# A linear-attention block beside a gated MLP on one core: the last down forms made in one K step, and x's second chunk loaded into their place

## The chip, the cores and the metric

The kernel runs on one core of one Trainium2 chip. The metric is device microseconds of one execution. Before the change three runs took 726.26, 726.73 and 728.23 us, so the median is 726.73.

## What is computed

x has 2048 rows of 640 columns. Two branches read it and a gate mixes them row by row. Cut to what matters, the reference is:

```python
def _A_ref(x, wqkv, wo):                      # H = 32 heads of Dh = 20
    q, k, v = split_heads(x @ wqkv)
    phi = lambda t: jnp.where(t > 0, t + 1, jnp.exp(t)) + 1e-6
    pq, pk = phi(q), phi(k)
    kv = jnp.einsum("bhsd,bhse->bhde", pk, v)
    z = jnp.einsum("bhsd->bhd", pk)
    num = jnp.einsum("bhqd,bhde->bhqe", pq, kv)
    den = jnp.einsum("bhqd,bhd->bhq", pq, z)[..., None] + 1e-6
    return merge_heads(num / den) @ wo

def _B_ref(x, w_gate, w_up, w_down):          # F = 1536
    return (_sigmoid(x @ w_gate) * (x @ w_up)) @ w_down

g = _sigmoid((x * gate_w).sum(-1, keepdims=True))
out = g * _A_ref(x, wqkv, wo) + (1 - g) * _B_ref(x, w_gate, w_up, w_down)
```

## The kernel before, in words

**Arithmetic.** Every large product is made from fp32 operands split in two: ScalarE (ACT) copies the operand to a rounded high half (L420), VectorE (DVE) subtracts it to get the low half (L424), and TensorE (PE) makes three matmuls, high by high, high by low and low by high (`mm3`, L407 to L409). The products of 2 by 2 blocks are made in seven steps rather than eight, so sums and differences of blocks of x and of the weights are needed; these are called forms. A block of the K or the Q product goes through steps s1 to s7. Its sums stand in PSUM tiles named ch, dd, cc and rot, two slots each: a product on a slot waits until ACT or DVE has copied or added what the slot held.

**Stages.** The K phase goes through four chunks of x's rows (c = 0 to 3): the K products, phi, and a batch that accumulates K transposed times x (`GTBatch`, tiles gt). It needs blocks of 128 rows of x as they stand (tiles xnst, split into tok) besides the transposed chunks. Then comes the q phase of the first pair of row groups: 16 steps, with the small products of the attention placed into it by a table, `extra[j]`, where `kv_part` (L1630) makes a head group's kv from gt and wv, and `m_part` (L1641) multiplies kv by wo in six 320-wide matmuls on dd or cc, copies them to ms and stores them to m_dram. phi of q is made in `phi_q` (Exp and Relu on ACT, one DVE operation into qe, a store to p_dram). Then come the f phase of the first pair (12 blocks of F), the down products, and the same q and f phases for the other pair.

**What sets the order.** The order of the work on every engine is the order of the program. Some of it is written out by hand, the rest is decided by a planner at build time (class `Order`): it keeps estimated clocks of PE, ACT and DVE and queues of pieces of work, and lets a piece go when its turn comes (`run`), when something due needs it (`need`), or when there is room (`fill`). Loads are issued on SyncE's queue (SP), stores on GpSimd's (POOL); both take their instructions in order and a transfer that has to wait for its tile holds up those behind it. ACT, DVE and PE also work in order.

**Around the change.** `queue_ls` (L755) queues under the key "qw" the work for the last pair's down weights: two steps of sums, then four forms (j = 0 and 1, two halves each), in tiles qraw and qp; after the second half of each j two stores to the buffer wd go out on POOL's queue. In the third K step (c = 3, L1131 to L1240) the sums are run after s5, one form at a time afterwards, and `need("qw")` runs the rest. Then the pool that held these tiles is closed, and in their place tile xz (tag ws) takes most of x's second chunk of the first pair (`nx[1].load`: xm, then two transfers to xz), behind it goes a load of q weights (wg from wq). `queue_xn` splits the last row blocks, and `split_xn` loads a new block into xnst after a split. Later the tag ws is also used for weight tiles of the q products.

Of the kernel before, what the change touches and what calls it, by code (L numbers as in the profile page):

```python
# [9 lines left out]
AF = mybir.ActivationFunctionType  # L10
# [364 lines left out]
def gated_mix_kernel(ctx: ExitStack, tc: tile.TileContext, xt, xn, wk, wv, wo, wst_q, wst_f, out_t):  # L375
# [6 lines left out]
    order = Order()  # L382
# [3 lines left out]
    def f32(ap):  # L386
        return ap.bitcast(F32)

    def width(ap):
        n = 1  # L390
        for s in ap.shape[1:]:
            n *= s
        return n
# [24 lines left out]
    def act(out, src, fn, after="", **kw):  # L418
        order.on_act(width(out), after, out, src)
        nc.scalar.activation(out, src, fn, **kw)  # L420
# [368 lines left out]
    def queue_qw(u):  # L789

        raw = qs.tile([P, 2, D], F32, name="qraw", tag="qraw")
        sp.dma_start(raw, wst_q[:, u:u + 2])
        g, v = raw[:, 0], raw[:, 1]
        w = 2 * P

        def piece(i, c, src):
            n = width(src)

            def fn():
                t = qs.tile([P, 2, w], F32R, name="qp", tag="qp", bufs=2)  # L800
                split(t[:, 0, :n], t[:, 1, :n], src)
                order.then(lambda: sp.dma_start(w_dram["q", u, i][:, :, c:c + n], f32(t[:, :, :n])))
            order.add(a_cost(n), v_cost(n), fn, "qw",
                      None, kept=True)

        for i, n in enumerate((D, 3 * P, 9 * P)):
            w_dram["q", u, i] = dram.tile([P, 2, n], F32, name=f"wq{u}{i}")
        for i, src, c0 in ((0, g, 0), (1, v, w)):
            for c in range(c0, D, w):
                piece(i, c - c0, src[:, c:min(c + w, D)])  # L810
        a11, a12, a21, a22 = g[:, :w], g[:, w:2 * w], v[:, :w], v[:, w:2 * w]
        g5, v5 = g[:, 2 * w:], v[:, 2 * w:]

        def sums(part):
            if part == 0:
                add(a22, a21, a22)
                sub(a21, a11, a21)
            else:
                sub(a11, a22, a11)
                sub(a12, a12, a11)  # L820
                sub(g5, g5, v5)
        for part in range(2):
            order.add(0, 2 * v_cost(w), lambda part=part: sums(part), "qw", None, kept=True)
        for n, t in ((7, a22), (0, a11), (5, a21), (2, a12), (4, g5)):
            piece(2, n * P, t)
# [24 lines left out]
    def queue_xn(b):  # L850
        for n in (2 * b, 2 * b + 1):
            order.add(a_cost(D), v_cost(D), lambda n=n: split_xn(n), ("xn", b), lambda n=n: xn_st[n][1])
# [278 lines left out]
    for c in range(1, 4):  # L1131
        ck = chunks[c]
        if c == 1:
            queue_qw(2)
        a, b = KBlock(2 * c), KBlock(2 * c + 1)
        for n in range(1, 6):
            order.need((ck, n))
            if c == 1 and n >= 3:
                order.need(("ks", (1, 0, 2)[n - 3]))
            getattr(a, f"s{n}")()  # L1140
            getattr(b, f"s{n}")()
            for _ in range(({1: 1, 2: 1, 3: 1, 5: 1}, {5: 2})[c - 2].get(n, 0) if c > 1 else 0):
                order.run("qw")
        order.need((ck, 6))
        if c == 1:
            order.need(("ks", 5))
        if c == 2:
            chunks[c + 1].load()
        elif c == 3:
            nx = [Chunk(1, i, None, i * CW, xst_v, (b12h, b12l)) for i in range(2)]  # L1150
            nx[0].load()
        if c == 1:
            order.need(("xn", 1))
        queue_xn(2 * c)
        a.s6()
        a.s7()
        a.sum_b()
        a.phi_a()
        if c == 3:
            order.run("qw")  # L1160
            order.run("qw")
        b.s6()
        a.phi_b()
        order.need(("pk", 2 * c - 1))
        k_split(tok(2 * c, 0))
        b.s7()
        b.sum_b()
        k_split(tok(2 * c, 1))
        if c == 3:
            order.need("qw")  # L1170
            qs_cm.__exit__(None, None, None)
            pa_cm.__exit__(None, None, None)
            px_cm = tc.tile_pool(name="px", bufs=1, side="right", reuse_waits="tile")
            px = px_cm.__enter__()
            xf = XForms(px, TG)
            pg_cm = tc.tile_pool(name="pg", bufs=1, side="right", reuse_waits="tile")
            pg = pg_cm.__enter__()
            pz_cm = tc.tile_pool(name="pz", bufs=1, side="right", reuse_waits="tile")
            pz = pz_cm.__enter__()
            z = pz.tile([P, 8, CW], F32, name="xz", tag="ws")  # L1180
            z0 = m1_tile("ma", "xm")[:, :2 * CW].rearrange("p (k c) -> p k c", c=CW)
            nx[1].x = (Rows((0, 2, z0), (2, KC, z[:, 0:3])), z[:, 3:8])
            nx[1].load(((0, 0, 2), (0, 2, KC), (1, 0, KC)))
            W, WT = {}, {}

            def wg_tile():
                return pg.tile([P, 2, D], F32R, name="wg", tag="wg", bufs=2)

            def put(n, i, t):
                WT[n, i] = t  # L1190
                W[n, i] = [t[:, c] for c in range(2)]

            def store_w(n, i):

                key = n[::2] + (i,)
                w_dram[key] = dram.tile(list(WT[n, i].shape), F32, name="w%s%d%d" % key)
                gp.dma_start(w_dram[key], f32(WT[n, i]))

            def wg_split(n, src):
                put(n, 0, wg_tile())  # L1200
                split(*W[n, 0], src)
                if n[0] == "f" or n[2] == 0:
                    order.then(lambda: store_w(n, 0))
            nx[0].f = nx[1].f = xf
            put(("q", 1, 2), 0, wg_tile())
            sp.dma_start(f32(WT[("q", 1, 2), 0]), w_dram["q", 2, 0])
        g = GTBatch(c, batches[c])
        if c > 1:
            order.need(("xn", 2 * c))
        if c == 1:  # L1210
            chunks[1].store_t(1, 0)
        elif c < 3:
            chunks[c + 1].queue()
        else:
            queue_xn(7)
        first = 4 if c == 1 else 3
        for u in range(first):
            g.part(u, 0, 2, ("rot", "dd", "ch", "cc")[u])
            if c == 1 and u == 0:
                order.need(("xn", 2))  # L1220
                chunks[1].store_t(2, 3)
                chunks[2].queue()
            if u == (c == 1):
                b.phi_a()
            if u == 1 + (c == 1):
                b.phi_b()
                order.ahead(5)
        queue_split(2 * c + 1)
        if c < 3:
            queue_xn(2 * c + 1)  # L1230
        else:
            w_stage = m1_tile("ma", "w0")
            sp.dma_start(w_stage, wst_q[:, KC - 1])
            queue_forms(nx)
        if c == 3:
            for u in range(first, NU):
                g.part(u, 0, 2, ("cc", "dd", "rot", "cc")[u - first])
                order.fill()
            freed = [order.pe + P_LAG]
        for u in range(NU):  # L1240
            g.part(u, 2 if u in g.ps else 0, 4, ("rot", "dd", "ch", "cc", "dd", "rot", "rot")[u])
            order.fill()
            if u in (2, 3, 4, 6):
                order.run("qw")
            if c == 2 and u == NU - 1:
                queue_ls()
# [188 lines left out]
    def phi_q(g, u, src, after="p"):  # L1435

        n = phis.pop() + 1
        phis.append(n)
        order.need(("den", n - 2))
        e = tt("qe")  # L1440
        act(e, src, AF.Exp, after)
        r = src if after == "v" else tt("qr")
        act(r, src, AF.Relu)

        def rest():
            vec3(e, e, 1.0, r, OP.min, OP.add)
            gp.dma_start(p_dram[:, u, g], e)
            if g < 2:
                order.add(0, v_cost(TG), lambda: den_term(g, u, e), ("den", n), chain=True)
        order.need("phi")  # L1450
        order.follow(v_cost(TG), rest, "phi")
# [1032 lines left out]
    extra[0] += [lambda: queue_wo(1), lambda: queue_wo(0)]  # L2484
    extra[7].append(lambda: order.need((nx[1], 6), False))
    extra[9].append(lambda: order.need(("w", ("q", 1, 0), 1), False))
    for hg, (j, t) in enumerate(((5, "cc"), (6, "dd"), (8, "dd"), (10, "dd"), (12, "dd"), (13, "dd"))):
        extra[j].append(lambda hg=hg, t=t: m_part(hg, t))
    for hg, j in ((3, 8), (4, 9), (5, 10)):
        extra[j].append(lambda hg=hg: order.need(("wo", hg), False))  # L2490
    extra[13].append(lambda: order.need(("wg", ("f", 1, 0)), False))
    extra[13].append(lambda: order.need(("w", ("f", 1, 0), 0), False))
# [571 lines left out]
```

## Time and profile before

The profile is one execution with the hardware profiler on.

| | |
|---|---|
| median of three runs | 726.73 us |
| the profiled execution's own time | 726.68 us |
| its span, first to last instruction | 725.0 us |
| instructions | 9883 |
| granted clock of TensorE | 1.00 |
| PE busy, share of the span | 718.9 us, 99% |
| weight loads (PEld) | 606.2 us, 84% |
| DVE | 583.1 us, 80% |
| ACT | 371.1 us, 51% |
| POOL | 116.8 us, 16% |

Busy time of PE is time in which a matmul runs; consecutive matmuls overlap a little, so their starts, and not their durations, tell what one costs. A row of a timeline gives the start in us, the duration, the engine, the line, the operation with what it writes and reads, and in brackets how long the engine stood idle before it and what released it.

### The profile page before, as it was taken

The numbers are of one execution on the slowest core, as the hardware profiler recorded it, in microseconds if no ns is written. First come the engines' busy times: TensorE is split into PE (matmuls) and PEld (weight loads), VectorE is DVE, ScalarE is ACT, GpSimd is POOL, SyncE is SP. The second block draws the span as 40 slices with busy tenths as digits, with TensorE's granted clock in tenths as the row PEclk, the third lists the DMA queues.
The fourth block names the chain that finished last, engine by engine and source line by source line (L and its number), as shares of the span: only waits on it lengthen the run. The fifth ranks groups of instructions, "written<-read, shape, count | busy, mean of one in ns | idle before, by whom it ended". The sixth has DMA issues, their size and how long they took to land.

```text
span 725.0 us, 9883 instructions
## 1 busy us (share of the span) xinstructions
PE 718.9 (99%) x3395; PEld 606.2 (84%) x3395; DVE 583.1 (80%) x1009; ACT 371.1 (51%) x685; POOL 116.8 (16%) x189
## 2 busy tenths in 40 slices
PE   9999999999999999999999999999999999999998
PEld 8999998887788888888888888888888888888887
DVE  6888878788677989898989977447696968799895
ACT  5774748267556753636363764354423242444451
POOL 0211013123221212210210134001010101002300
PEclk9999999999999999999999999999999999999999
DMA  7677677978777866767687889968989895959957
GB/s 253 165 201 210 179 179 199 330 263 288 287 276 257 322 237 242 258 222 261 258 311 274 276 294 354 412 232 287 350 262 305 260 394 178 407 215 332 221 104 237
DMA packets 78889, 191.95 MB, mean 265 GB/s; under 512 B 8394, under 2 KB 37018, under 8 KB 75126
## 3 DMA queue, kind: packets, MB, share of 16 engines
q1 hardware_dynamic: 57654, 117.72, 49.2%
q0 software_dynamic: 20896, 73.36, 30.3%
q8 instruction: 27, 0.44, 0.2%
q10 hardware_dynamic: 288, 0.23, 0.1%
q14 instruction: 24, 0.20, 0.1%
HBM read 113.46 MB, written 75.52 MB: 261 GB/s over the span
## 4 chain that ended last, share of the span: by engine, by line
PE 91%; DMA 3%; issue 2%; DVE 2%; POOL 1%; ACT 1%; POOLq 0%; ACTq 0%; DVEq 0%
PE ch L407 10%; PE ch L408 10%; PE ch L409 10%; PE cc L407 8%; PE cc L408 8%; PE cc L409 8%; PE dd L407 6%; PE dd L408 6%; PE dd L409 6%; PE rot L407 5%; PE rot L409 5%; PE rot L408 5%; DMA wst<-wst_f 2%; DMA wst<-wst_q 1%; DMA p_dram<-qe 1%
## 5 line engine op out<-in xcount | busy, mean ns | idle before, releaser
L420 ACT ACTIVATE c<-ch 128x512 f32<-128x512 f32 x54 | 32.2, 596 | 80.1 <-PE ch L409 79.3
L424 DVE TENSOR_TENSOR hf<-c,hf 128x512 fp32r<-128x512 f32 x80 | 54.4, 686 | 19.4 <-ACT hf L420 18.9
L420 ACT ACTIVATE hf<-c 128x512 fp32r<-128x512 f32 x80 | 48.9, 624 | 31.1 <-DVE c L424 31.0
L424 DVE TENSOR_TENSOR c<-cc,c 128x512 f32<-128x512 f32 x42 | 28.9, 688 | 26.1 <-PE cc L409 16.6
L407 PE MATMUL ch<-xth,ws 128*128 128x512 f32 x112 | 43.9, 392 | 0.1
L408 PE MATMUL ch<-xtl,ws 128*128 128x512 f32 x112 | 43.7, 390 | 0.0
L409 PE MATMUL ch<-xth,ws 128*128 128x512 f32 x112 | 43.6, 389 | 0.0
L424 DVE TENSOR_TENSOR c<-c,c 128x512 f32<-128x512 f32 x52 | 35.7, 687 | 3.3 <-ACT c L420 2.7
L424 DVE TENSOR_TENSOR tb<-rot,tb 128x512 f32<-128x512 f32 x56 | 36.1, 680 | 0.4 <-PE rot L409 0.4
L407 PE MATMUL dd<-xrh,wg 128*128 128x512 f32 x90 | 35.2, 391 | 0.0
L408 PE MATMUL dd<-xrl,wg 128*128 128x512 f32 x90 | 35.0, 389 | 0.0
L409 PE MATMUL dd<-xrh,wg 128*128 128x512 f32 x90 | 35.0, 389 | 0.0
L420 ACT ACTIVATE c<-dd 128x512 f32<-128x512 f32 x22 | 13.1, 597 | 41.1 <-PE dd L409 41.1
L407 PE MATMUL cc<-xbh,ws 128*128 128x512 f32 x84 | 32.8, 390 | 0.5 <-DVE c L424 0.5
L408 PE MATMUL cc<-xbl,ws 128*128 128x512 f32 x84 | 32.7, 389 | 0.0
L409 PE MATMUL cc<-xbh,ws 128*128 128x512 f32 x84 | 32.7, 389 | 0.0
L424 DVE TENSOR_TENSOR tb<-dd,tb 128x512 f32<-128x512 f32 x36 | 24.7, 685 | 9.3 <-PE dd L409 9.3
L420 ACT ACTIVATE dd<-ch 128x512 f32<-128x512 f32 x22 | 12.8, 582 | 35.9 <-PE ch L409 35.9
L424 DVE TENSOR_TENSOR tb<-cc,tb 128x512 f32<-128x512 f32 x36 | 24.4, 683 | 1.9 <-PE cc L409 1.9
L424 DVE TENSOR_TENSOR wst<-wst 128x256 f32<-128x256 f32 (+1 forms) x65 | 24.6, 395 | 1.4
L407 PEld LDWEIGHTS ch<-xth,ws 128*128 128x128 f32 x112 | 21.0, 188 | 5.0 <-ACT c L420 0.9
L409 PEld LDWEIGHTS ch<-xth,ws 128*128 128x128 f32 x112 | 21.0, 188 | 4.7 <-DVE ws L424 0.3
(690 smaller groups left out, 2328.5 us busy)
## 6 DMA issues: line engine op xcount, KB each, us to landing
wf<-ws POOLq DMA_DIRECT2D x12, 1152.0 KB, 7.6
ws<-wf SPq DMA_DIRECT2D x11, 1152.0 KB, 7.8
wst<-wst_f SPq DMA_DIRECT2D x12, 640.0 KB, 5.3
wf<-wg POOLq DMA_DIRECT2D x12, 640.0 KB, 7.2
wd<-wd POOLq DMA_DIRECT2D x12, 640.0 KB, 7.8
wg<-wf SPq DMA_DIRECT2D x12, 640.0 KB, 6.6
wf<-wd SPq DMA_DIRECT2D x10, 640.0 KB, 10.4
xnst<-xn SPq DMA_DIRECT2D x16, 320.0 KB, 3.2
```

The costliest lines, as they stand in the source:

```text
L407: nc.tensor.matmul(out, l_hi, r_hi, start=first, stop=False, skip_group_check=True)
L408: nc.tensor.matmul(out, l_hi, r_lo, start=False, stop=False, skip_group_check=True)
L409: nc.tensor.matmul(out, l_lo, r_hi, start=False, stop=last, skip_group_check=True)
L420: nc.scalar.activation(out, src, fn, **kw)
L424: nc.vector.tensor_tensor(out, a, b, op=op)
```

## The change

Four places change.

1. In the third K step the queue "qw" is run four times after s5, not twice: the two sums and the first two forms (j = 0) follow each other.
2. The other two forms (j = 1) are run right after block a's s6 instead of after its `phi_a`.
3. In `phi_q`, when the source has been added by DVE (`after == "v"`), the planner is no longer told that Exp waits for DVE. That is a clock of the planner alone; the instruction still waits for its data.
4. m_part 5 moves from extra step 13 to 14, and the need for its wo block from step 10 to 11.

```diff
-            for _ in range(({1: 1, 2: 1, 3: 1, 5: 1}, {5: 2})[c - 2].get(n, 0) if c > 1 else 0):
+            for _ in range(({1: 1, 2: 1, 3: 1, 5: 1}, {5: 4})[c - 2].get(n, 0) if c > 1 else 0):
                 order.run("qw")
...
         a.s6()
+        if c == 3:
+            order.run("qw")
+            order.run("qw")
         a.s7()
         a.sum_b()
         a.phi_a()
-        if c == 3:
-            order.run("qw")
-            order.run("qw")
         b.s6()
...
-        act(e, src, AF.Exp, after)
+        act(e, src, AF.Exp, "" if after == "v" else after)
...
-    for hg, (j, t) in enumerate(((5, "cc"), (6, "dd"), (8, "dd"), (10, "dd"), (12, "dd"), (13, "dd"))):
+    for hg, (j, t) in enumerate(((5, "cc"), (6, "dd"), (8, "dd"), (10, "dd"), (12, "dd"), (14, "dd"))):
         extra[j].append(lambda hg=hg, t=t: m_part(hg, t))
-    for hg, j in ((3, 8), (4, 9), (5, 10)):
+    for hg, j in ((3, 8), (4, 9), (5, 11)):
         extra[j].append(lambda hg=hg: order.need(("wo", hg), False))
```

The order of the engines' instructions changes in several places, because the planner decides anew with every change of its clocks. On POOL's queue in the third K step, the stores of the forms (wd from qp and qraw) stand between accumulating stores of phi(k) (zacc from kr and kb); rows with - are the order before, with + the order now:

```order
 L364 DMA zacc<-kb 128x2x320
-L364 DMA zacc<-kr 128x2x320
 L364 DMA wd_1157<-qp 128x512
 L364 DMA wd_1157<-qraw 128x512
-L364 DMA zacc<-kb 128x2x320
 L364 DMA wd_1157<-qp 128x512
 L364 DMA wd_1157<-qraw 128x512
 L364 DMA zacc<-kr 128x2x320
 L364 DMA zacc<-kb 128x2x320
+L364 DMA zacc<-kr 128x2x320
+L364 DMA zacc<-kb 128x2x320
```

The four stores of the forms are now together, ahead of the four accumulating stores. On SP's queue, behind the first chunk's loads (xst), x's second chunk (xm and xz) stood behind the last row block (xnst), and ahead of the q weights (wg) and a weight stage (w):

```order
 L364 DMA xst<-xt 128x5x256 x2
-L364 DMA xnst<-xn 128x640
 L364 DMA xm<-xt 128x2x256
 L364 DMA xz<-xt 128x3x256
 L364 DMA xz<-xt 128x5x256
 L364 DMA wg<-wq_468 128x1280
+L364 DMA xnst<-xn 128x640
 L364 DMA w_1422<-wst_q 128x640
```

The last row block is now loaded behind the second chunk and the q weights. On PE near the end of the first pair's q phase, block B's s5 (ch from xth and ws), m_part 5 (dd from woh, wol and kv) and the first products of its s6 (ch from xth, xtl and wu) stood like this before:

```order
L407 MATMUL ch_1764<-xth,ws 128x512
L408 MATMUL ch_1764<-xtl,ws 128x512
L409 MATMUL ch_1764<-xth,ws 128x512
L407 MATMUL dd_2042<-woh,kvh 100x320
L408 MATMUL dd_2042<-wol,kvh 100x320
L409 MATMUL dd_2042<-woh,kvl 100x320
L407 MATMUL dd_2047<-woh,kvh 100x320
L408 MATMUL dd_2047<-wol,kvh 100x320
L409 MATMUL dd_2047<-woh,kvl 100x320
L407 MATMUL ch_1764<-xth,wu 128x512
```

And now, at the end of s6 and the start of s7 (cc from xbh and ws):

```order
L407 MATMUL ch_1756<-xrh,wu 128x512
L408 MATMUL ch_1756<-xrl,wu 128x512
L409 MATMUL ch_1756<-xrh,wu 128x512
L407 MATMUL dd_2060<-woh,kvh 100x320
L408 MATMUL dd_2060<-wol,kvh 100x320
L409 MATMUL dd_2060<-woh,kvl 100x320
L407 MATMUL dd_2065<-woh,kvh 100x320
L408 MATMUL dd_2065<-wol,kvh 100x320
L409 MATMUL dd_2065<-woh,kvl 100x320
L407 MATMUL cc_2000<-xbh,ws 128x512
```

The six matmuls of m_part 5 stand between s6 and s7 now, and s6 follows s5 directly on the same ch tile. On ACT and DVE the changes are these: the splits of the forms directly follow their sums; the splits of row blocks 12 and 13 (tok from xnst) stand behind the split of the K results; form 3, that is two sums and two low halves (xst, xz, then xtl) in the q phase, stands behind block B's addition from dd (c from dd), where it stood ahead of it; the Exps and their stores to p_dram shift by a place or two. The number of matmuls is the same.

## The prediction

> **What bounds the kernel now.** I read the page's first part, then the busy time in three stretches, then the timeline of TensorE (PE) at each place where it starts late.
>
> ```profile
> span 725.0 us, 9883 instructions
> PE 718.9 (99%) x3395; PEld 606.2 (84%) x3395; DVE 583.1 (80%) x1009; ACT 371.1 (51%) x685; POOL 116.8 (16%) x189
> ```
>
> PE is busy 99% of the span, and the change adds or removes no matmul. So it can act only on the time in which PE stands. The stretches (us, then busy time of PE, weight loads, DVE, ACT and POOL, the granted clock, the DMA share, GB/s) say where that is:
>
> ```profile
> 12.00:143.00 131.00, 131.00 (x751) 120.92 (x750) 108.53 (x199) 80.69 (x163) 22.79 (x25) 1.00 0.76 207
> 143.00:194.00 51.00, 49.12 (x258) 40.51 (x257) 40.26 (x79) 35.06 (x64) 15.50 (x29) 1.00 0.84 294
> 194.00:720.00 526.00, 526.00 (x2327) 434.55 (x2326) 427.60 (x716) 247.46 (x441) 78.32 (x132) 1.00 0.81 278
> ```
>
> Before 143 us and behind 194 us PE has no gap, at a granted clock of 1.00. All that can be won lies between, in the q phase of the first pair and the head of its f phase, and anything below can only be lost elsewhere. I price each gap from one start to the next, less the usual spacing, and add what the next spacing is too long.
>
> First gap, PE waiting for DVE's add c<-dd (block B's product on dd):
>
> ```profile
> 159.00 0.31 PE L408 MATMUL dd<-wol,kvh 120*120 120x320 f32 x1
> 159.15 0.31 PE L409 MATMUL dd<-woh,kvl 120*120 120x320 f32 x1
> 160.05 0.41 PE L407 MATMUL dd<-woh,kvh 120*120 120x320 f32 x1 [0.59 <-DVE c L424]
> 160.29 0.31 PE L408 MATMUL dd<-wol,kvh 120*120 120x320 f32 x1
> ```
>
> A 320-wide matmul follows its neighbour by 0.15. The gap is 0.90 - 0.15 = 0.75, and the restart 0.24 - 0.15 = 0.09: 0.84 us. Second, for the low half of wo:
>
> ```profile
> 165.80 0.31 PE L407 MATMUL dd<-woh,kvh 100*100 100x320 f32 x1
> 166.56 0.39 PE L408 MATMUL dd<-wol,kvh 100*100 100x320 f32 x1 [0.45 <-DVE wol L424]
> 166.79 0.31 PE L409 MATMUL dd<-woh,kvl 100*100 100x320 f32 x1
> ```
>
> 0.61 + 0.08 = 0.69 us. Third and fourth, around block B's s5, m_part 5 and s7:
>
> ```profile
> 178.50 0.39 PE L408 MATMUL ch<-xtl,ws 128*128 128x512 f32 x1
> 178.72 0.40 PE L409 MATMUL ch<-xth,ws 128*128 128x512 f32 x1
> 179.39 0.39 PE L407 MATMUL dd<-woh,kvh 100*100 100x320 f32 x1 [0.27 <-DVE ms L868]
> 179.62 0.31 PE L408 MATMUL dd<-wol,kvh 100*100 100x320 f32 x1
> ```
>
> ```profile
> 182.19 0.39 PE L409 MATMUL ch<-xrh,wu 128*128 128x512 f32 x1
> 183.06 0.50 PE L407 MATMUL cc<-xbh,ws 128*128 128x512 f32 x1 [0.47 <-DVE c L424]
> 183.39 0.40 PE L408 MATMUL cc<-xbl,ws 128*128 128x512 f32 x1
> ```
>
> A 512-wide one follows by 0.22 to 0.23. The third costs 0.67 - 0.23 + 0.08 = 0.52, the fourth 0.87 - 0.23 + 0.10 = 0.74. The last two stand at the head of the f phase:
>
> ```profile
> 188.40 0.39 PE L409 MATMUL dd<-xrh,wg 128*128 128x512 f32 x1
> 188.79 0.50 PE L407 MATMUL ch<-xth,ws 128*128 128x512 f32 x1
> 189.13 0.40 PE L408 MATMUL ch<-xtl,ws 128*128 128x512 f32 x1
> ```
>
> ```profile
> 192.13 0.39 PE L409 MATMUL cc<-xbh,wu 128*128 128x512 f32 x1
> 192.62 0.50 PE L407 MATMUL ch<-xth,ws 128*128 128x512 f32 x1
> ```
>
> 0.16 + 0.11 = 0.27, and 0.26 with the same restart of 0.11, 0.37. All six together: 0.84 + 0.69 + 0.52 + 0.74 + 0.27 + 0.37 = 3.43 us. That is the most that the change can gain.
>
> **The forms made together.** The additions and splits of the last pair's down weights stay as many as before, and DVE has no gap there that PE waits for. What moves is the time at which their tiles come free for x's second chunk.
>
> ```profile
> 109.89 1.79 DVE L424 TENSOR_TENSOR qraw<-qraw 128x256 f32<-128x256 f32 x4
> ```
>
> ```profile
> 120.06 1.07 POOL L364 DMA_DIRECT2D wd<-qp  x1
> 120.62 1.07 POOL L364 DMA_DIRECT2D wd<-qraw  x1
> ```
>
> ```profile
> 125.32 0.99 SPq L364 DMA_DIRECT2D xz<-xt  x2
> 126.40 1.54 SPq L364 DMA_DIRECT2D wg<-wq  x1
> ```
>
> The sums are done at 111.7. Before, the last of the four stores was issued at 120.62, and xz 4.70 later, when it had landed. Now the four lows follow the sums at once (a quarter of 1.79 each at most, so until 113.5 at the latest; I take 113.1), and the stores follow each other on POOL at 0.56, as the two above, with no accumulating store between them, the last at about 113.9. With a landing in 3.4 to 4.7 us, xz goes out at 117.3 to 118.6. I take 117.6, 7.7 us sooner. The accumulating stores (zacc) now stand behind the four; nobody waits for them here but the next of their kind.
>
> But SP's queue also changed: the last token block (xnst) is now issued behind xz and wg, where it went out ahead of them.
>
> ```profile
> 130.57 0.84 ACT L420 ACTIVATE xrh<-xz 128x768 fp32r<-128x768 f32 x1 [4.04 <-DMA xz<-xt]
> ```
>
> ```profile
> 134.83 0.74 ACT L420 ACTIVATE wg<-w 128x640 fp32r<-128x640 f32 x1 [1.03 <-DMA w<-wst_q]
> ```
>
> The last of the three loads landed at about 134.75, 9.4 us after xz's issue. The token block takes that place, so it lands at 117.6 + 9.4 = 127.0. ACT works in order, and its split of that block stands ahead of every split of x's chunk. ACT's 4.04 us of waiting for xz therefore becomes waiting for xnst: the chunk lies ready sooner, but is split from about 127.9 on and not from about 120.
>
> ```profile
> 122.50:128.24 5.74, 5.74 (x29) 4.78 (x28) 5.74 (x9) 4.03 (x7) 1.25 (x1) 1.00 0.77 157
> ```
>
> ```profile
> 158.09 0.69 DVE L424 TENSOR_TENSOR xtl<-xst,xth 128x512 fp32r<-128x512 f32 x1
> 158.70 0.69 DVE L424 TENSOR_TENSOR xtl<-xz,xth 128x512 fp32r<-128x512 f32 x1
> 159.31 0.68 DVE L424 TENSOR_TENSOR c<-dd,c 128x512 f32<-128x512 f32 x1
> ```
>
> DVE worked without a gap until 128.24 on what now waits for the block, so it resumes about as much work behind (5.74) as it lacked before. What relieves it is the planner's new order: form 3 (two sums and two lows, 4 x 0.60 = 2.40 us by the starts above) now stands behind B's c<-dd add. The add then ends at about 159.2 instead of 159.99. PE would be ready for it at 159.15 + 0.15 = 159.30. So **the first gap goes: -0.84**, with 0.1 us to spare. The low half of wo is now made right behind that add, where before it stood behind the kv blocks, and **the second gap goes: -0.69**. What DVE's chain slips beyond that comes back one for one.
>
> What is late next is form 3 itself. Between the add and the end of its last low, DVE's order now has two sums, two lows and a qe (5 x 0.60), a wol and a wg (640 wide, 0.75 by their width) and two kv blocks, which took 1.51 in this stretch:
>
> ```profile
> 164.18:165.69 1.51, 1.51 (x8) 1.24 (x7) 1.37 (x7) 1.51 (x3) 1.33 (x3) 1.00 0.23 47
> ```
>
> 3.00 + 1.50 + 1.51 = 6.0 behind 159.2 is 165.2. The tile ws that block A's s6 needs takes the place of xz, so ACT splits ws only then.
>
> ```profile
> 166.00 0.60 ACT L420 ACTIVATE c<-ch 128x512 f32<-128x512 f32 x1 [0.17 <-PE ch L409]
> ```
>
> Two ws splits by 640 and 512 columns (1.15 together, 0.74 being the time of one of 640), and behind them the 0.60 copy of ch on ACT's queue, for which PE's next ch product waits: 165.2 + 1.15 + 0.60 + 0.1 = 167.05. A's s6 started here:
>
> ```profile
> 168.19 0.48 PE L407 MATMUL ch<-xth,wu 128*128 128x512 f32 x1
> ```
>
> Less the two gaps gone, 168.19 - 0.84 - 0.69, PE is there at 166.66. **A new wait: +0.40, with the restart +0.50.** It is an estimate from below and above: nothing if the chain ends 0.4 sooner, 1.5 if it ends a microsecond later.
>
> **m_part 5 one step later.** The six matmuls stay; they now follow s6, not s5. The third and fourth gap (0.52 + 0.74 = 1.26) are replaced by one: s6 follows s5 on the same ch tile, and must wait for ACT's copy. By the rows above: 0.40 of the last matmul, 0.04, 0.60 of the copy, 0.05, less the spacing of 0.23, is 0.86; with a restart of 0.10 it is 0.96. The six matmuls (6 x 0.15 = 0.9) then cover DVE's add ahead of s7. **-1.26 + 0.96 = -0.30.** Between +0.2 (cc still waits) and -0.75 (ACT copies in two parts of the last product's time) I take the sum.
>
> **Exp without the planner's wait** takes no wait out of the program: the data still decide. It lets the planner put Exp and its store earlier on ACT and POOL.
>
> ```profile
> 186.95 0.63 ACT L420 ACTIVATE qe<-c 128x512 f32<-128x512 f32 x1 [1.64 <-DMA p_dram<-qe]
> ```
>
> This Exp held ACT's queue for 1.64 us until a store had landed, and behind it stood the copies for which the fifth and sixth gap waited. If that store goes out 1.64 us sooner, nothing is left of the wait. It stands a store sooner on POOL's queue now, behind one less Exp, which I put at 2 to 3.5 us sooner: **-0.64**, and 0 at the least.
>
> The sum: -0.84 - 0.69 + 0.50 - 0.30 - 0.64 = -1.97, taken as -1.95. The profiled execution took 726.68 (span 725.0 and 1.68 around it), the median of the runs is 726.73, so the sum is carried over as it is: 726.73 - 1.95 = 724.8.
>
> **The rivals.** *More is won.* The new wait for ws falls away because the chain is 0.4 us early, or s6 waits less: -2.5 to -2.9, 723.8 to 724.2. For it: each of the two is a matter of 0.4 us, less than my landings are certain to. Against it: both need ACT free at a given moment, and ACT's queue is what got longer there.
>
> *It is given back.* The chunk lands early and is split late, the add still ends behind 159.9, and form 3 behind it delays ws: the first gap stays (0.84) and the ws wait is a full one: -0.3 to -1.1, 725.6 to 726.4. This is also the case in which the change does not do what it says: the load is sooner, what is made from it is not. For it: the token split now ahead of the chunk on ACT.
>
> *Slower: the token block is late.* Its transposes are in PE's order:
>
> ```profile
> 131.36 0.34 PE L407 MATMUL rot<-tok 128*128 128x384 f32 x1
> ```
>
> They need the block landed, split by ACT and DVE (0.74 and about as much) and its handover, so landed by about 129.2. The forecast has 127.0, 2.2 us of cover where before it went out ahead of xz. If the wd stores land as late as they did (xz at 125.32), it lands at 134.7 and PE stands 5.5 us in a stretch that has no gap today, less the 1.95 won: +3.5, 730.2. The point from which it costs more than it brings is a slip of 2.2 + 1.95 = 4.2 us; 6.3 us for a loss of 0.3%. For it: three transfers, xm, xz and wg, are now ahead of the block in SP's queue. Against it: only the four stores, with no accumulating one among them, stand between the lows and xz.
>
> The Trainium skill has two rules that speak for this rival. "TensorE: Matmul & The Clock Gate", Part 1 (What's actually happening), says that an idle window of about 3.4 us halves the clock; the waits here are all below 0.9 us with a granted clock of 1.00, so no run here shows it, and by it a 5.5 us wait would cost about 1.7 us on top, an estimate from that page: 731.9. "DMA: Bandwidth & Descriptors", Queues, rings and completion order, says that each DMA engine takes turns between queues by packet; by it xz and the block would share with the zacc stores that now follow, which in the trace would show as landings later than mine.
>
> **How the numbers follow.** A measurement of this kernel can tell a difference of about 0.3%, 2.2 us, from none. Chances: the forecast (-1.2 to -2.4) 0.48, more won 0.25, given back 0.17, slower 0.10. Faster by over 0.3% is the case of more won and a quarter of the forecast's: 0.38. Slower by over 0.3% is most of the last case: 0.08. The rest, 0.54, is within. The range leaves out the slow case and the edges of the two nearest ones: 723.9 (-2.8) to 727.0 (+0.3, a token block just late).
>
> **What would show it.** Right: xz issued at about 117.6; PE without gaps at 159 and 166 in block B's first steps; one gap of about 0.9 between s5 and s6, none ahead of s7; xz's first split behind the split of the last tokens. Wrong: a gap of PE before 143 us (the token block), a gap at the first ch product of A's s6 beyond 0.5, Exp still waiting for p_dram near 187, or any gap behind 194 us.

## The result, and the profile after

| | before | after |
|---|---|---|
| median of the runs beside each other | 726.59 us (4 runs) | 732.62 us (4 runs) |
| ratio, 95% interval | | 1.0078, 1.0054 to 1.0101 |
| profiled execution, its span | 726.68, 725.0 us | 731.44, 729.7 us |

The kernel became slower by about 6 us; 724.8 was forecast, and 732.62 lies outside the range of 723.9 to 727.0. The page after says that the work is the same:

```profile
span 729.7 us, 9894 instructions
PE 719.4 (99%) x3395; PEld 606.6 (83%) x3395; DVE 583.2 (80%) x1009; ACT 370.3 (51%) x685; POOL 117.0 (16%) x189
```

The stretches (columns as before) say where the time went. Up to 143 us PE now stands a little, and between 143 and 200 it stands 5.84 us at a granted clock of 0.97; behind 200 nothing has changed:

```profile
12.00:143.00 131.00, 130.65 (x744) 119.94 (x743) 105.55 (x195) 80.42 (x163) 21.86 (x25) 1.00 0.77 209
143.00:200.00 57.00, 51.16 (x264) 43.01 (x263) 44.32 (x86) 35.41 (x65) 17.14 (x31) 0.97 0.81 270
200.00:725.00 525.00, 525.00 (x2323) 433.76 (x2322) 426.62 (x714) 246.84 (x440) 77.80 (x131) 1.00 0.81 278
```

PE's waits (us in total, times, longest) hold a long one that was not there. The four of before are gone; in their place stand ACT's copy for ch (0.5 and 0.7 us) and the token block (0.4).

```profile
PE rot L407 <- DVE kvt L424: 4.6, 1, 4.6
```

The timeline of PE at the long wait shows what comes with it:

```profile
148.63 0.39 PE L409 MATMUL dd<-xah,wg 128*128 128x512 f32 x1
153.66 0.47 PE L407 MATMUL rot<-xbh,wg 128*128 128x512 f32 x1 [4.64 <-DVE kvt L424]
...
154.30 0.63 PE L409 MATMUL rot<-xbh,wg 128*128 128x512 f32 x1
154.73 0.63 PE L407 MATMUL rot<-xbh,wg 128*128 128x512 f32 x1
```

5.03 us from start to start, less the usual 0.23, is 4.80. Behind it the matmuls take 0.63 instead of 0.39 and follow each other by 0.43, not 0.23; the granted clock of that stretch, 0.55, is the third number from the end:

```profile
153.70:157.30 3.60, 3.60 (x10) 2.81 (x11) 3.43 (x9) 0.65 (x2) 0.00 (x0) 0.55 1.03 275
```

Until the spacing is back at 157.6 the slow clock costs 1.65 us more. The chain of waits gives the reason in one piece (start, duration, what):

```profile
119.26 9.71 DMA xnst<-xn
...
130.81 10.69 DMA zacc<-kr
...
142.03 6.35 DMA zacc<-kb
```

The last two accumulating stores of phi(k) land at 141.5 and 148.4. ACT's split of wo's first block, which the planner now puts ahead of the splits of x's new sums, writes a tile (woh) in the place of the one (kb) that the last store still reads. ACT waits, and DVE behind it with all its queue, the kv blocks that PE needs among it:

```profile
148.46 1.36 ACT L420 ACTIVATE woh<-wo_sb 120x640 fp32r<-120x640 f32 x2 [6.36 <-DMA zacc<-kb]
```

```profile
149.23 1.56 DVE L424 TENSOR_TENSOR wol<-wo_sb,woh 120x640 fp32r<-120x640 f32 x2 [5.43 <-ACT woh L420]
```

Before, nothing held that split; ACT came to it later, 6.8 us behind the last store's landing at 138.1:

```profile
144.90 0.73 ACT L420 ACTIVATE woh<-wo_sb 120x640 fp32r<-120x640 f32 x1
```

POOL's four stores to zacc then went out like this:

```profile
113.92 1.19 POOL L364 DMA_DIRECT2D zacc<-kr  x1 [11.94 <-DVE kr L428]
...
119.31 1.22 POOL L364 DMA_DIRECT2D zacc<-kb  x1 [3.06 <-DMA zacc<-kr]
...
124.20 1.25 POOL L364 DMA_DIRECT2D zacc<-kr  x1 [2.52 <-DVE tok L428]
130.33 1.21 POOL L364 DMA_DIRECT2D zacc<-kb  x1 [4.87 <-DMA zacc<-kr]
```

And after:

```profile
114.22 1.22 POOL L364 DMA_DIRECT2D zacc<-kr  x1 [0.60 <-DVE logit L868]
120.09 1.19 POOL L364 DMA_DIRECT2D zacc<-kb  x1 [4.65 <-DVE logit L868]
130.81 1.21 POOL L364 DMA_DIRECT2D zacc<-kr  x1 [9.53 <-DVE tok L424]
142.03 1.19 POOL L364 DMA_DIRECT2D zacc<-kb  x1 [10.01 <-DVE xst L424]
```

Each adds to the same tile and so waits for the one before to land. For the last two the brackets name a DVE instruction, but the stores ahead of them landed at 130.1 and 141.5, 0.7 and 0.5 us before these went out, as the second follows the first's landing by 0.6: it is the landing that let them go. The first goes out at nearly the same time in both. The second took 4.9 us until the next could go, and now 10.7; the third 6.1, and now 11.2. SP's queue after says what is in the air with them:

```profile
117.38 1.08 SPq L364 DMA_DIRECT2D xz<-xt  x2
118.51 0.65 SPq L364 DMA_DIRECT2D wg<-wq  x1
119.26 0.38 SPq L364 DMA_DIRECT2D xnst<-xn  x1
122.01 0.33 SPq L364 DMA_DIRECT2D w<-wst_q  x1
130.60 0.33 SPq L364 DMA_DIRECT2D wst<-wst_q  x1
```

Before, the second store flew beside two wd stores of the forms alone (DMA share 0.65, 125 GB/s between 119.3 and 123.4; xz left at 125.32), the third went out 1.1 us ahead of xz, and the fourth 1.2 us ahead of the next burst (wst at 131.56, three wv, two wo and more); it landed in 7.8 us, at 138.1. Now the second goes out 2.7 us behind xz (DMA share 0.82, 232 GB/s between 120.1 and 130.1) and the third 0.2 us behind the start of the second burst.

The token block costs something too:

```profile
131.38 0.44 PE L409 MATMUL rot<-tok 128*128 128x384 f32 x1 [0.35 <-DVE tok L428]
```

The whole account, from PE's starts: the token block +0.96 (0.52 for DVE's part of the block at 131.38 and four slow restarts of 0.11), the wait +4.80, the slow clock +1.65, the gaps that were to go -3.43, what stands in their place +1.70. That is +5.68. The profiled execution of before was 0.96 slower in its first 8 us, so the spans differ by 4.7; the medians by 6.0. This also means that up to 130 us the rows of before stand about 0.95 late against those of after (PE's first transpose of the last token block: 131.36 and 130.41); the token block takes that away, and from 133 on both stand on the same time.

### The profile page after: what moved, and what is told of

It is laid out like the page before. It is cut to its first block, busy times and chain, and to the rows that moved or that the text cites. A ratio compares the mean times of both kernels' runs of the same rounds, so it can differ in the third digit from the quotient of the medians.

```text
span 729.7 us, 9894 instructions
## 1 busy us (share of the span) xinstructions
PE 719.4 (99%) x3395; PEld 606.6 (83%) x3395; DVE 583.2 (80%) x1009; ACT 370.3 (51%) x685; POOL 117.0 (16%) x189
## 4 chain that ended last, share of the span: by engine, by line
PE 92%; DMA 4%; ACT 2%; DVE 1%; issue 1%; ACTq 0%; DVEq 0%; POOLq 0%
PE ch L407 11%; PE ch L408 11%; PE ch L409 11%; PE cc L407 8%; PE cc L408 8%; PE cc L409 8%; PE dd L407 6%; PE dd L408 6%; PE dd L409 6%; PE rot L407 5%; PE rot L409 5%; PE rot L408 5%; DMA zacc<-kr 1%; DMA xnst<-xn 1%; DMA zacc<-kb 1%; PE dd L2789 1%
## 5 line engine op out<-in xcount | busy, mean ns | idle before, releaser
L407 PE MATMUL ch<-xth,ws 128*128 128x512 f32 x112 | 43.6, 390 | 0.0
L408 PE MATMUL ch<-xtl,ws 128*128 128x512 f32 x112 | 43.6, 390 | 0.0
L407 PE MATMUL dd<-xrh,wg 128*128 128x512 f32 x90 | 35.2, 391 | 0.0
L408 PE MATMUL dd<-xrl,wg 128*128 128x512 f32 x90 | 35.0, 389 | 0.0
L407 PE MATMUL cc<-xbh,ws 128*128 128x512 f32 x84 | 32.7, 389 | 0.0
L408 PE MATMUL cc<-xbl,ws 128*128 128x512 f32 x84 | 32.7, 389 | 0.0
L420 ACT ACTIVATE dd<-ch 128x512 f32<-128x512 f32 x22 | 12.8, 582 | 35.9 <-PE ch L409 35.9
L409 PEld LDWEIGHTS ch<-xth,ws 128*128 128x128 f32 x112 | 21.0, 188 | 4.7 <-DVE ws L424 0.3
L408 PEld LDWEIGHTS ch<-xtl,ws 128*128 128x128 f32 x112 | 21.0, 188 | 4.3
```

The source lines that it names most:

```text
L407: nc.tensor.matmul(out, l_hi, r_hi, start=first, stop=False, skip_group_check=True)
L408: nc.tensor.matmul(out, l_hi, r_lo, start=False, stop=False, skip_group_check=True)
L409: nc.tensor.matmul(out, l_lo, r_hi, start=False, stop=last, skip_group_check=True)
```

## The experiments

Theory A is the story above: the stores' chain, lengthened by the loads that now fly with it, holds a tile that wo's split needs. Its rivals are B, the other two edits; C, the token block that lands late and DVE's work behind it; and D, that accumulating is slow by itself. The first four kernels were run beside the same runs of before (726.11), the next four beside 726.18, the next three beside 725.90, the last beside 726.06.

**The first two edits alone.**

```diff
-  {5: 2}
+  {5: 4}
...
   a.s6()
+  if c == 3: order.run("qw"); order.run("qw")
...
   a.phi_a()
-  if c == 3: order.run("qw"); order.run("qw")
```

> The kernel before with the forms made together and run earlier (the first two edits), and nothing else of the change. Theory A: the loss comes from the accumulating stores zacc. The second of them now flies beside x's second chunk, lands about 6 us later and pushes the third and fourth into the next burst of loads; the first high half of wo reuses the tile that the last store reads, ACT waits for it until 148.4 us, DVE behind ACT, and PE behind DVE for 4.8 us. Then this kernel loses as the whole change does: PE waits 4 to 5 us near 149, 732 to 734 us. Theory B: the loss comes from the other edits (Exp placed earlier by the planner, m_part 5 later): 726 to 727 us here.

731.97 us, ratio 1.0085 (1.0072 to 1.0098). The whole loss is in the forms, and the wait is the same one:

```profile
PE rot L407 <- DVE kvt L424: 5.4, 1, 5.4
```

**The other edits alone.**

```diff
-  act(e, src, AF.Exp, after)
+  act(e, src, AF.Exp, "" if after == "v" else after)
...
-  (12, "dd"), (13, "dd")
+  (12, "dd"), (14, "dd")
```

> The kernel before with only Exp without the planner's wait and m_part 5 a step later. The orders of SP and of POOL in the K phase are those of before. Theory A: no long wait near 149; gap of 0.95 between s5 and s6 in place of 1.26, and the two gaps at the head of the f phase shorter: 725.6 to 726.5 us. Theory B: 731 us or more.

726.20 us, ratio 0.9999 (0.9990 to 1.0008): theory B falls. A gain does not show in the medians either, though the interval would allow 0.7 us. The gap between s5 and s6 was expected at 0.95 and is not:

```profile
PE ch L407 <- ACT c L420: 1.1, 1, 1.1
```

With m_part 5 gone from between them, s6 waits 1.1 us for ACT's copy of s5, and not the 0.69 of the changed kernel: 1.26 from the starts and a restart of 0.11, so 1.37 where the two gaps of before cost 1.26. ACT, still at ws, starts that copy 0.87 us behind the start of s5's last matmul, and 0.43 behind it in the changed kernel. The move of m_part 5 wins nothing by itself. At the head of the f phase 0.39 is left of 0.64.

**The changed kernel without the last two accumulating stores.**

```diff
-  gp.dma_start(zacc, r, accum_op=...)
+  gp.dma_start(zacc, r, skip=len(z_started) >= 14, accum_op=...)
```

> The changed kernel without the last two accumulating stores of phi(k), so the sum of keys lacks two of its sixteen row blocks; the planner's clocks and so the order of everything else are those of the changed kernel. Theory A: ACT splits wo's first high half as soon as ch is copied, near 142 to 143 us, DVE goes on without its idle 5.4 us, the wait of PE of 4.8 us and the slow clock behind it (1.6 us more) are gone: 725 to 726.7 us. Theory C: the token block that lands late, and DVE's work that it pushes back, makes the wait; then PE still waits 4 us or more near 149: 731 to 733 us.

726.07 us, ratio 0.9999 (0.9990 to 1.0007). PE's waits (this kernel has one line more, so L408 here is L407 elsewhere):

```profile
PE ch L408 <- ACT c L421: 0.7, 1, 0.7
PE dd L408 <- DVE c L425: 0.6, 1, 0.6
PE rot L408 <- ACT tok L421: 0.6, 1, 0.6
PE rot L410 <- DVE tok L429: 0.3, 1, 0.3
```

The long wait is gone with the stores, and the order of everything else is as in the changed kernel. Theory C does not make it. What C does make is in the last two lines, the token block, and in the second: c<-dd is late again, by 0.79 and a restart of 0.10, as before the change.

**The changed kernel with wo's first splits queued later.**

```diff
-  extra[0] += [lambda: queue_wo(1), lambda: queue_wo(0)]
+  extra[2] += [lambda: queue_wo(1), lambda: queue_wo(0)]
```

> The changed kernel with all its stores; the splits of the first two blocks of wo are queued in extra step 2 and not 0, so that the sums of x, the kv blocks and block A's addition from dd stand ahead of them on ACT and DVE. Theory A: the last zacc store still lands near 148, but only the wo splits wait for it: no wait of PE above 1 us near 149, 725 to 727 us. Theory C: as the changed kernel, 731 to 733 us.

728.00 us, ratio 1.0021 (1.0011 to 1.0031). Of the loss of 6.0 us 1.9 are left, and the forecast of 725 to 727 is missed:

```profile
PE cc L407 <- DVE kvt L424: 1.5, 1, 1.5
PE ch L407 <- ACT c L420: 1.1, 2, 0.7
PE dd L407 <- DVE c L424: 1.1, 1, 1.1
```

A tile of the kv blocks also lies over a stored one, so part of the wait came back through DVE's cast (kvh, 2.08 us idle for the last store, which landed at 149.2), and c<-dd is again late.

**Copies in place of accumulations.**

```diff
-  accum_op=OP.add if z_started else OP.bypass
+  accum_op=OP.add if z_started and len(z_started) < 12 else OP.bypass
```

> The changed kernel, order and all, but the last four stores to zacc copy and do not accumulate (the sum of keys is then wrong), while each still waits for the one before. Tells what makes the second of them take 10 us where it took 5. Theory A (they share the DMA engines with the burst of loads that now flies at the same time): the second is still issued at 120 and lands near 130, ACT still waits for the last until about 148; time about 732 us. Theory D (the accumulation, a read and a write of the same place, is what is slow): copies land in 3 to 5 us each, the last near 135, no wait near 149, about 726 us.

726.18 us (one run), no long wait, as D had it, and not the 732 that A forecast. POOL's second, third and fourth store:

```profile
119.46 0.73 POOL L364 DMA_DIRECT2D zacc<-kb  x1 [4.21 <-DVE logit L868]
129.16 0.72 POOL L364 DMA_DIRECT2D zacc<-kr  x1 [8.97 <-DMA zacc<-kb]
132.41 0.72 POOL L364 DMA_DIRECT2D zacc<-kb  x1 [2.53 <-DVE tok L428]
```

A plain copy behind the burst of xz takes 9.7 us as well until the next can go, so sharing is enough for that (A). The third then goes out at 129.16, ahead of the second burst (130.91 here), and is through in 3.3 us at most. The fourth goes out 1.5 us behind the burst's start and lands in 7.1, where accumulating stores at that place took 10.7 to 12.8: accumulating has a share too (D). Both theories were half right. The third left 1.65 us sooner than in the changed kernel, 0.63 because the second did and 1.0 because the copy was quicker, and that put it ahead of the second burst.

**Both losses taken away: token block first, last two stores left out.**

```diff
   if c == 3:
+      order.need(("xn", 2 * c))
       order.need("qw")
...
+  skip=len(z_started) >= 14
```

> The changed kernel with both suspected losses taken away: the last row block is loaded ahead of x's second chunk (row blocks 12 and 13 are split before the queue of forms is emptied), and the last two accumulating stores are left out (the sum of keys lacks two row blocks). Tells whether the gains that were forecast for the q phase are there. If they are (first and second gap gone, s5 to s6 at 0.95, none in the f phase): 724 to 725 us. If the gains were never there: 726 us or more.

724.05 us, ratio 0.9973 (0.9962 to 0.9984). The gains that were forecast exist. PE's starts at the place of the first gap (one line more here too):

```profile
159.26 0.31 PE L410 MATMUL dd<-woh,kvl 120*120 120x320 f32 x1
159.42 0.41 PE L408 MATMUL dd<-woh,kvh 120*120 120x320 f32 x1
159.67 0.30 PE L409 MATMUL dd<-wol,kvh 120*120 120x320 f32 x1
```

Nothing but the restart of 0.10 is left of it; the second gap is gone, between s5 and s6 stand 0.96, at the head of the f phase 0.30: 1.36 of 3.43 us, a gain of 2.1.

**Token block first, xz held until the second store has landed.**

```diff
+  held = dram.tile([1, 64], F32, name="held")
+  nc.sync.dma_start(held, zacc[:1, :64])
   nx[1].load(...)
```

> The changed kernel with the last row block first, and with a small transfer (64 numbers of zacc to a scratch place) ahead of x's second chunk on SP's queue, which must wait until the second accumulating store has landed: so x's chunk and what is behind it start at about 125 as before the change, and everything else keeps the changed order. Theory A: the second accumulating store lands in about 5 us, by 125, the fourth goes out by 133 and ACT splits wo by 144; no wait above 1 us near 149; 725 to 727 us. If the order of POOL's stores or the planner's new order of DVE is the cause: PE still waits 4 us near 149, 731 us or more.

730.66 us, ratio 1.0062 (1.0044 to 1.0080), PE's long wait 5.8 us. The second store did land in under 5 us (4.1, at 123.3), but theory A's next step failed. SP and POOL:

```profile
124.26 1.00 SPq L364 DMA_DIRECT2D xz<-xt  x2
```

```profile
125.17 1.21 POOL L364 DMA_DIRECT2D zacc<-kr  x1 [4.79 <-DVE tok L428]
136.59 1.19 POOL L364 DMA_DIRECT2D zacc<-kb  x1 [10.21 <-DMA zacc<-kr]
```

With xz at about its old time, the third store went out 0.9 us behind it and took 11.4 us; before the change it went out 1.1 us ahead of it and took 6.1. So it is not the early hour of xz by itself, but when a store goes out against the loads. That corrects the theory. The experiment had a hand in it: here the third store left 1.9 us behind the second's landing, not 0.5 to 0.8 as in the other kernels with all four stores. The added transfer reads the tile that the third writes, which would explain it, but this was not tried apart.

**A version with all its stores: token block first, wo's splits in step 3.** The edits are those above, with `extra[3]`.

> A version with all its stores that should lose neither: the changed kernel with the last row block loaded first and the first two splits of wo queued in extra step 3. Theory A: the token wait of PE (0.8 to 0.95 us) is gone, the wo splits come after the last store has landed; what the kv tiles, that also take places of the stored tiles, wait for may remain: 725 to 727 us. Otherwise 728 us or more.

729.45 us, ratio 1.0044 (1.0032 to 1.0056): missed. The stores again obey the order against the second burst (131.15 here; POOL):

```profile
127.73 1.21 POOL L364 DMA_DIRECT2D zacc<-kr  x1 [7.07 <-DMA zacc<-kb]
133.29 1.19 POOL L364 DMA_DIRECT2D zacc<-kb  x1 [4.35 <-DVE gt L424]
```

The third goes ahead of it, in 5.6 us; the fourth, 2.1 us behind its start, lands only after 12.8. But the splits of wo, put off, now hold up PE themselves (1.1 and 0.7 us for wol), and ACT's copy is late for s6:

```profile
182.05 0.75 PE L407 MATMUL ch<-xth,wu 128*128 128x512 f32 x1 [1.98 <-ACT c L420]
182.60 0.63 PE L408 MATMUL ch<-xtl,wu 128*128 128x512 f32 x1
```

The clock is halved here too (granted 0.51 between 182.1 and 185.6, starts 0.43 apart), behind a wait of 1.98 us.

**Two merged stores instead of four, with token block first, with the change alone, and without the change.** In the K phase's last two blocks the two halves are added and stored once:

```diff
-  z_add(dst)
-  z_add(k)
+  zs = kr_tile("zs")[:, :, :HALF]
+  add(zs, KR[tok(self.b, 0)], k)
+  z_add(zs)
```

> A repaired version that computes everything: the changed kernel with the last row block loaded ahead of x's second chunk, and, for the last two blocks of the K phase, phi(k) of a block's two halves added by DVE into one free tile of the same ring and stored once, so two accumulating stores stand in the chain instead of four (two additions of 640 columns more on DVE, about 0.75 us each, in a stretch where DVE waits for loads). If the chain of stores behind the bursts of loads is the cause: the second store goes out near 124 and lands near 132, no wait near 149, no wait for the token block; as the run with both losses taken away (724.05), 723.5 to 725.5 us. If something else in the changed order costs the time: 728 us or more.

> The changed kernel with the merged stores, the last row block still loaded behind x's second chunk. Theory: the wait near 149 is gone, the token wait of about 1 us near 131 stays: 1 to 1.7 us above the repaired version, 725 to 726.5 us.

> The control: the kernel before with only the two merged stores of the last two K blocks, none of the change. If merging the stores pays by itself, 724 to 725 us; by the theory the chain of stores ends at 138 there, well ahead of its first reader at 144.9, so nothing is won: 725.8 to 727 us (the planner's order shifts a little).

The repaired version takes 724.69, ratio 0.9985 (0.9977 to 0.9994): faster than before, with no long wait, as expected. The change with merged stores and the token block last takes 727.42, ratio 1.0017 (1.0007 to 1.0027): missed by 1 us. Two of PE's waits there, which the repaired version does not have:

```profile
PE dd L407 <- DVE c L424: 1.0, 1, 1.0
...
PE rot L1636 <- DVE gt L424: 0.7, 1, 0.7
```

The two differ in the place of one 320 KB load, and by 2.7 us. The token block pushes all of DVE's work back, and what it costs shows in the q phase, where c<-dd is late again, and not only at the transposes.

The control went the other way than expected: the kernel before with nothing but merged stores takes 723.81, ratio 0.9970 (0.9958 to 0.9981), the fastest of all and 0.9 us faster than the repaired version. Beside it, the change itself brings nothing. SP's second chunk:

```profile
121.94 0.98 SPq L364 DMA_DIRECT2D xz<-xt  x2
```

That is 3.4 us sooner than 125.32, 0.7 of it because the profiled execution of before started slowly (the loads of xst left at 106.01, and at 105.34 here). Before, POOL's queue held the second pair of wd stores behind a zacc store that waited 3.06 us for the one before it (119.31 above). With one zacc store less, that wait does not stand in the queue: the last wd store goes out at 118.89, not 120.62, and xz follows it by 3.05 us, not 4.70. The forms' tiles come free without any form being moved. The first four gaps are gone, one of 0.86 at the head of the f phase is left.

**That version with Exp moved as well.** The third edit on top of the merged stores.

> The kernel before with the two merged stores (723.81 by themselves) and, of the change, only Exp without the planner's wait. What is left there is a gap of 0.76 and its restart of 0.10 at the head of the f phase, where ACT's Exp waits 2.54 us for a store to p_dram. The theory: with Exp and its store a place sooner that gap goes, 722.8 to 723.6 us; if the wait for the store only moves, 723.8 to 724.8.

724.35 us, ratio 0.9974 (0.9963 to 0.9985): the wait only moved. PE now stands 1.2 us for a copy of m_part:

```profile
PE dd L407 <- DVE ms L869: 1.2, 1, 1.2
```

```profile
176.55 0.69 DVE L428 SCALAR_TENSOR_TENSOR qe<-qe,c 128x512 f32<-128x512 f32 x1 [0.49 <-DMA p_dram<-qe]
...
178.52 0.88 DVE L869 COPY ms<-dd 100x320 f32<-100x320 f32 x2
```

The copy stands in DVE's queue behind a qe that waits for a store to p_dram; without the Exp edit it stood ahead of that qe, at 175.21.

## Right and wrong, step by step

**Wrong, the step that decided.** "The accumulating stores (zacc) now stand behind the four; nobody waits for them here but the next of their kind." The order of POOL's queue hardly moved them (the first left at 114.22, 113.92 before, which is 1.3 us later once the slow start of before is taken off). But each had room before only because the bursts of loads came behind it, and somebody does wait for the last: the split that writes wo's high half over the tile it reads. Before, the chain ended 6.8 us ahead of that split (138.1 against 144.90); now ACT is ready for it at 142.1 and the chain ends at 148.4. The trace puts 4.80 us and 1.65 of slow clock on it, and without the last two stores both are gone. The prediction looked at who reads zacc, and not at who next writes the tiles that the stores read. The sentence on DVE, that what slips "comes back one for one", had the mechanism but not this cause.

**Mis-sized, the token block.** It was a rival, with its end at 129.2. xz left at 117.38 (forecast 117.6; on the clock of before's profile 118.3, still within 117.3 to 118.6). The block landed 11.6 us behind xz, at 128.97, and not 9.4 behind it; the second store flew in the same stretch. On the clock of before's profile that is 129.9, so the cover was overrun by 0.7 us, and PE lost 0.96. With all that follows the late block costs 2.0 us (the runs without the last two stores, 726.07 and 724.05) to 2.7 (the two merged versions): the cover was counted to PE's next transposes alone, and not to DVE's queue.

**Right in mechanism.** The first two gaps go when the stores are out of the way (1.53 us forecast, 1.43 measured in the run without them and with the token block first). Between s5 and s6: 0.96 forecast, 0.95 in the changed kernel. The sum of -1.95 was -2.1 there. The wait for ws at A's s6 was forecast at 0.50: it is 0.75 in the changed kernel and nothing in that run. So the sum came out in part by luck: 0.50 that did not come stands against 0.30 less won in the f phase and the 0.10 left of the first gap.

**Mis-sized, the f phase.** It was to win 0.64; in that run 0.34 was won, and 0.25 by the last two edits alone. On top of the merged stores the gap at its head went, and a wait of 1.40 at m_part 5 came instead.

**The rivals.** "Slower: the token block is late" named the right queue and the wrong transfer, with a price of 730.2; its chance of 0.10 was too low, because a rival with stores and loads in the same stretch was read from one side only, loads waiting for stores. "It is given back" (725.6 to 726.4) describes the changed kernel once the stores are out of the way: 726.07, the chunk split late, the first gap back. So without the stores the gain of 1.95 would not have come either. (The chance of faster by over 0.3% adds up to 0.37, not 0.38.) Two rules were named beside the slower case.

The Trainium skill, "TensorE: Matmul & The Clock Gate", Part 1 (What's actually happening), says that an idle window of about 3.4 us halves the clock. The prediction's estimate from it was 1.7 us behind a long wait, and 1.65 were measured behind 4.64 us. The wait of 1.98 us that also halved the clock is shorter than the 3.4 that it gives; here the measurement decides.

"DMA: Bandwidth & Descriptors" of the Trainium skill, Queues, rings and completion order, would have a store and loads take turns by packet. The stores did take about twice as long beside a burst. But while the second and the third were in flight in the changed kernel, SP's queue moved 1098 and 885 packets and POOL's 272 each time (120.1 to 130.1, 130.8 to 141.5); beside the fourth it was 371 and 324, a store of gt_dram among them (142.0 to 148.4). Only the last looks like equal turns, if the profile's packets are the ones meant.

By the moment of issue the landings form a slope and not a switch. Against the start of the second burst (wst), 3.4 us ahead a store landed in 5.0, 1.2 ahead in 7.8, 0.5 ahead in 8.1, 0.2 behind in 10.7, 0.6 behind in 11.3 and 2.1 behind in 12.8. Yet 11.4 behind, with the DMA engines as busy as before (share 1.05), it landed in 6.4. So full engines alone are not what slows a store.

What stays open: what the DMA engines do with a store behind the first loads of a burst, and how much accumulating adds to it. No run has one store and one load by themselves.

## What to carry to other kernels

Before moving a load earlier, list the transfers that are in the air at its new time, follow each to the next writer of the tile it reads, and count how much room that has; in a chain of transfers that wait for each other, what each loses adds up. When a queue in front of a stalled engine is in order, look for the entry in it that waits: taking one waiting store out of POOL's queue brought the same load forward by about 2.7 us, for two additions on DVE. A gap that goes is worth only what the next engine in line leaves of it: try each edit alone.

## What the runs showed of the hardware

From 113 us on, a 320 KB accumulating store to zacc on POOL's queue landed in 4.1 to 8.1 us when it was issued half a microsecond or more ahead of SP's burst (counted from the nearer of xz and wst), and in 7.3 to 12.8 us when it was issued between 0.1 us ahead of its start and six microseconds behind it; later than that, in 6.0 to 9.5. A plain copy landed in 2.7 us when it was issued 1.75 us ahead, and in 9.1 and 7.1 us behind (one run). After waits of PE of 4.64, 5.4 and 5.8 us, and once of 1.98 us, the matmuls ran at about half speed for some 3 to 4 us; after waits of 1.5 us and less they did not.
